# Exponentials over three PSUM banks, and the planner's queues made anew around them, in a fused attention and spectral filter kernel

## Chip, cores and metric

The kernel runs on one core of a Trainium2 chip. The metric is the time of one execution on the device in microseconds (us). TensorE is called PE below, ScalarE ACT, VectorE DVE, GpSimd POOL and SyncE, which issues most DMAs, SP.

## What is computed

Two independent halves, written side by side into one output of 2048 x 1280:

```python
# A: filter in the frequency domain, x is (1, 2048, 640)
X = rfft2(x.astype(float32))
y = irfft2(X * (w_r + 1j * w_i), s=(S, D)).astype(bfloat16)

# B: attention, 32 heads of 20, sequence 2048
qkv = (x @ wqkv).reshape(B, S, 3, H, Dh).transpose(2, 0, 3, 1, 4)
scores = einsum("bhqd,bhkd->bhqk", q, k) * Dh ** -0.5
o = einsum("bhqk,bhkd->bhqd", softmax(scores), v)
out_b = o.transpose(0, 2, 1, 3).reshape(B, S, D) @ wo
```

## The kernel before

**Tiles.** Attention goes in 32 units: 4 blocks of 512 queries times 8 groups of 4 heads. A unit has 64 tiles of scores, 16 blocks of 128 keys times 4 heads, 2048 in all. A tile is one matmul of 128 keys by 512 queries over 20 (padded to 32) rows, `score_mm` (L880), and fills one of the eight PSUM banks. The four heads of a group lie in four row groups of the PE array, so that tiles of different heads can be computed side by side, in one wave. The exponential of a tile is taken by one of two engines:

- ACT takes it exactly, two tiles in two neighbouring banks in one instruction of 128 x 1024 (L1615), into a ring of 22 slots in SBUF.
- DVE takes it by a bit trick: an eviction of 128 x 512 (or of a pair, 128 x 1024) into int16 (L1052), then for a batch of four tiles two passes over 128 x 2048 (L1110, L1113) and a scaling of V for that batch (L1102 on POOL, L1104 on DVE).

The products with V (L1198, "PV") come in waves of four matmuls, one per head, and a batch of DVE needs three waves where four tiles of ACT need one. Fills and all other products use different tile shapes of the PE array (32 rows by 128 columns against 128 rows by 32 columns).

**Around it** run the projections (L654 and, through the helper `cmm`, L283), the filter's matrix products in four stages (S1 to S4, L283), the normalisation, the output projection, their evictions on DVE, and POOL's additions. At the end an accuracy flag is read; a branch behind it holds a fallback that isn't executed here. It is the same in both kernels.

**Order.** Nothing is scheduled at run time. The class `KB` plans the program while it is built: `run` steps a clock of estimates, and whenever an engine is free by that clock it gives it the next piece. `step_pe1` tries, in this order, a fill for ACT (`try_act_fill`), background products (`bg_continue`, `bg_resume`, `try_bg`), PV waves (`try_pv`) and a fill for DVE alone (`try_dve_fill`). Where none fits, `keep_warm` may add a matmul with the identity that serves nothing else. `Prog` then works out the semaphores, and each engine executes its queue in order.

**Banks.** `SETS` gives ACT two pairs of banks, filled and emptied by turns; `POOLB` lists the other four, shared by DVE's tiles, by PV sums and by all background products (`bank_owner`). `try_act_fill` takes two tiles, and, where DVE has little to do, puts one or two tiles for DVE into the same wave, into shared banks. The exponential is issued in `try_exp`:

```python
SETS = ((0, 1), (2, 3))
POOLB = (4, 5, 6, 7)
...
in_ = self.ps[:, banks[0]:banks[0] + n, :].rearrange("p b n -> p (b n)")
self.put("act", lambda e: e.activation(o, in_, AF.Exp, bias=ACT_BIAS, scale=ACT_SCALE), ...
```

**Thresholds.** `POLICY` is a list of rows, each with a planner time in ns from which its values hold: how much work DVE may have waiting when it gets another tile (`DVE_BACK`, `DVE_BACK2`, and `DVE_LOW` for a fill of its own), how many PV matmuls make a group (`VMIN`), and the like (`NAMES`).

Of the kernel before, what the change touches and what calls it, by code (L numbers as in the profile page):

```python
# [260 lines left out]
NU = 32  # L261
# [45 lines left out]
class KB:  # L307
# [10 lines left out]
    SETS = ((0, 1), (2, 3))  # L318
    POOLB = (4, 5, 6, 7)
# [598 lines left out]
    DMIN = 14  # L918
# [15 lines left out]
    def try_act_fill(self):  # L934
        if self.ua >= NU:
            return False
        banks = self.SETS[self.grp]
# [4 lines left out]
        if self.P.peek("pe", w=[("ps", b) for b in banks]) > self.now:  # L942
            return False
        tiles = self.pick_set(len(banks))
# [4 lines left out]
        if self.dq and self.dve_wants(0):  # L949
            for k in (2, 1):  # L950
                alt = self.pick_set(len(banks), [t[2] for t in self.dq[:k]])
                if len(alt) == len(banks) and len({t[:2] for t in self.aq + alt}) <= 2:
                    tiles = alt
                    break
        left = sum(4 * len(q) for q in self.qs[self.ua:self.ua + 2]) + len(self.aq)
# [4 lines left out]
        bl = banks[:len(tiles)]  # L960
        rk = set()
# [35 lines left out]
        return True  # L997

# [8 lines left out]
    SOON = 1400.0  # L1007
    GGAP = 6000.0
    gat_next = 0.0
    RSV = 1200.0  # L1010
# [473 lines left out]
    def try_bg(self, room, urgent=False):  # L1484
        if not urgent and any(J.nxt < len(J.pe) for J in self.flight):
            return False
        banks = self.POOLB if self.act_started and self.ua < NU else (4, 5, 6, 7, 0, 1, 2, 3)
# [34 lines left out]
    def emit_chunk(self, J):  # L1522
# [11 lines left out]
        if J.nxt == len(J.pe):  # L1534
# [12 lines left out]
            self.dve_push(ops, done, any_=any_)  # L1547
# [52 lines left out]
    def try_exp(self):  # L1600
# [25 lines left out]
    NAMES = ('DVE_BACK', 'DVE_BACK2', 'VMIN', 'DVE_LOW', 'BMIN', 'PRP', 'DMIN', 'VGAP', 'RSH', 'SOON', 'RSV')  # L1626
    POLICY = [
# [876 lines left out]
```

## Time and profile before

| | |
|---|---|
| median of 3 runs | 713.07 us (713.04 to 713.34) |
| the profiled execution | 713.46 us |
| its span in the trace | 711.6 us |
| busy share: PE, DVE, ACT, POOL | 98%, 95%, 97%, 44% |
| exponentials on ACT | 748 of two tiles: 1496 tiles |
| tiles on DVE | 552, in 138 batches |

The profile comes from one execution, and its span is shorter than the time of that execution by what lies around the program. A busy time counts an engine as busy from an instruction's start to its end, and successive instructions overlap in it. So a stretch that is all busy can still hold losses: there the distance from one start to the next says more.

### The profile page before, as it was taken

What the parts mean: (1) busy time and instruction counts of PE and PEld (TensorE: products, weight loads), DVE (VectorE), ACT (ScalarE), POOL (GpSimd) and SP (SyncE); (2) the same over time, 40 slices, a digit from 0 to 9 for tenths busy, and PEclk for the clock granted to TensorE, in tenths of its full rate; (3) what the DMA queues carried; (4) which work ended last, traced back from release to release, by engine and by line L of the source; (5) the groups of instructions that cost most, each with busy time, mean ns of one, the idle gap of its engine ahead of it and who ended that gap; (6) DMA issues with size and microseconds to landing.
All of it is one profiled execution on the core that took longest, in us unless ns stands there. A gap on an engine that the chain in (4) does not pass through costs nothing.

```text
span 711.6 us, 24028 instructions
## 1 busy us (share of the span) xinstructions
PE 697.5 (98%) x10275; PEld 224.9 (32%) x10275; DVE 674.2 (95%) x1227; ACT 690.8 (97%) x754; POOL 313.3 (44%) x322
## 2 busy tenths in 40 slices
PE   8999999999999999999999999999999999999997
PEld 3422342433422222223233333333222322233333
DVE  2799999999999999999999999999999999999996
ACT  4999999999999999999999999999999999999994
POOL 6364432122343313135126177676555325658660
PEclk9999999999999999999999999999999999999999
DMA  9522222212213427133211111110300120022211
GB/s 168 183 67 73 70 68 63 62 30 60 58 31 94 137 81 266 28 111 92 58 44 32 60 32 40 37 46 19 112 21 25 38 69 19 11 72 58 75 43 50
DMA packets 54292, 48.07 MB, mean 68 GB/s; under 512 B 27884, under 2 KB 45678, under 8 KB 53926
## 3 DMA queue, kind: packets, MB, share of 16 engines
q1 hardware_dynamic: 51526, 44.36, 22.2%
q8 instruction: 82, 1.34, 0.8%
q0 software_dynamic: 768, 1.32, 0.8%
q10 hardware_dynamic: 1888, 0.81, 0.5%
q14 instruction: 28, 0.23, 0.1%
HBM read 26.67 MB, written 11.76 MB: 54 GB/s over the span
## 4 chain that ended last, share of the span: by engine, by line
ACT 63%; PE 33%; DMA 1%; DVE 1%; SPq 0%; issue 0%
ACT arena L1615 63%; PE ps L880 12%; PE ps L283 11%; PE ps L1198 9%; PE ps L654 1%; DMA arena<-in_B_x_dram 1%; DMA arena<-in_B_wqkv_dram 1%; DVE arena L1052 0%; SPq L591 0%; PE ps L1310 0%; DVE arena L1434 0%; DVE arena L1380 0%; DVE arena L2260 0%; PE ps L1293 0%; DVE arena L1110 0%
## 5 line engine op out<-in xcount | busy, mean ns | idle before, releaser
L1615 ACT ACTIVATE arena<-ps 128x1024 f16<-128x1024 f32 x748 | 687.5, 1097 | 8.4 <-PE ps L880 8.2
L1052 DVE TENSOR_SCALAR arena<-ps 128x512 int16<-128x512 f32 (+1 forms) x546 | 363.1, 688 | 11.4 <-PE ps L880 9.5
L880 PE MATMUL ps<-arena 32*128 32x512 bf16 x2048 | 293.2, 384 | 5.9 <-ACT arena L1615 3.7
L1198 PE MATMUL ps<-arena 128*32 128x512 f16 x3152 | 262.2, 384 | 1.0 <-DVE arena L2128 0.5
L283 PE MATMUL ps<-arena 128*32 128x512 bf16 (+7 forms) x4758 | 253.2, 307 | 0.4 <-DMA arena<-in_B_wqkv_dram 0.2
L880 PEld LDWEIGHTS ps<-arena 32*128 32x128 bf16 x2048 | 72.5, 91 | 275.7 <-ACT arena L1615 259.9
L1102 POOL TENSOR_SCALAR arena<-arena 128x96 bf16<-128x96 bf16 x95 | 59.9, 631 | 145.9 <-DVE arena L1052 104.0
L283 PEld LDWEIGHTS ps<-arena 128*32 128x32 bf16 (+2 forms) x4758 | 89.2, 95 | 98.8 <-issue 68.7
L1113 DVE TENSOR_SCALAR arena<-arena 128x2048 int16<-128x2048 int16 x138 | 94.3, 686 | 1.1 <-PE ps L1198 0.9
L1110 DVE TENSOR_SCALAR arena<-arena 128x2048 int16<-128x2048 int16 x138 | 94.4, 684 | 0.2
L1198 PEld LDWEIGHTS ps<-arena 128*32 128x32 bf16 x3152 | 62.6, 95 | 93.1 <-issue 60.3
L1249 POOL TENSOR_TENSOR arena<-arena 128x512 bf16<-128x512 f32 x30 | 44.6, 1487 | 61.9 <-DVE arena L1052 41.1
L2144 POOL TENSOR_TENSOR arena<-arena 128x644 bf16<-128x644 bf16 x32 | 47.2, 1477 | 15.9 <-DVE arena L1052 9.1
L1903 POOL TENSOR_TENSOR arena<-arena 128x319 bf16<-128x319 f32 x16 | 16.4, 1026 | 27.4 <-DVE arena L1110 11.8
L2128 DVE TENSOR_TENSOR arena<-ps,arena 128x644 bf16<-128x644 f32 (+1 forms) x34 | 27.9, 820 | 0.4 <-PE ps L283 0.3
L2223 POOL TENSOR_TENSOR arena<-arena 128x512 bf16<-128x512 f32 (+1 forms) x12 | 17.5, 1456 | 20.3 <-DVE arena L2215 19.6
L1897 POOL TENSOR_TENSOR arena<-arena 128x640 f32<-128x640 bf16 x8 | 12.3, 1541 | 31.3 <-DVE arena L744 14.6
L664 DVE TENSOR_SCALAR arena<-ps,arena 128x512 bf16<-128x512 f32 (+1 forms) x14 | 10.2, 731 | 13.9 <-PE ps L654 13.9
L1904 POOL TENSOR_TENSOR arena<-arena 128x319 bf16<-128x319 f32 x16 | 15.3, 956 | 17.9 <-DVE arena L1052 5.2
L701 DVE TENSOR_SCALAR arena<-ps 128x512 bf16<-128x512 f32 x34 | 23.1, 680 | 0.0
L1229 DVE COPY arena<-ps 128x512 f32<-128x512 f32 (+1 forms) x33 | 21.9, 667 | 0.7 <-PE ps L1198 0.6
L2280 POOL TENSOR_TENSOR arena<-arena 128x321 bf16<-128x321 f32 x16 | 16.2, 1013 | 10.6 <-DVE arena L2260 8.3
(62 smaller groups left out, 244.7 us busy)
## 6 DMA issues: line engine op xcount, KB each, us to landing
arena<-rd SPq DMA_DIRECT2D x120, 64.0 KB
out_dram<-arena SPq DMA_DIRECT2D x30, 160.0 KB
arena<-in_A_x_dram SPq DMA_DIRECT2D x16, 160.0 KB
xs<-arena SPq DMA_DIRECT2D x16, 160.0 KB
arena<-xs SPq DMA_DIRECT2D x4, 640.0 KB
arena<-arena SPq DMA_DIRECT2D x105, 20.0 KB
qsv<-arena SPq DMA_DIRECT2D x8, 256.0 KB
arena<-ct SPq DMA_DIRECT2D x2, 1024.0 KB
```

The lines of the kernel that those rows point to most:

```text
L283: inst = e.matmul(out[c:c + n], lhsT[:, c:c + n], rhs, start=start, stop=stop, tile_position=(0, c), skip_group_check=True)
L701: return lambda e, en: e.tensor_scalar(o, in_, sc, None, ALU.mult)
L880: return e.matmul(self.ps[:, bank, :], self.KT[32 * j:32 * j + 32, g, kt * 128:(kt + 1) * 128], self.QT[32 * j:32 * j + 32, g, qc % 2 * 51 ...
L1052: return e.tensor_scalar(o, in_, 0.0, 31744.0, ALU.max, ALU.min)
L1102: self.pool_op(lambda e: e.tensor_scalar(vs, vi, W1, None, ALU.mult), 430.0, r=vr, w=vk, name="vs")
L1110: return lambda e, en=None: e.tensor_scalar(Gi[:, lo:hi], Ii[:, lo:hi], SH1, 0.0, ALU.subtract, ALU.max)
L1113: return e.tensor_scalar(Ii, Ii, SH2, 0.0, ALU.subtract, ALU.max)
L1198: inst = e.matmul(self.ps[32 * j:32 * j + 32, bank, :], v_, p_, start=s_, stop=False, tile_position=(0, 32 * j), skip_group_check=True)
L1249: self.pool_op(lambda e: e.tensor_tensor(on, of, bc, ALU.mult), 1250.0, r=pk + [("bcu", u, j) for j in range(4)] + [("bc", j) for j in ran ...
L1615: self.put("act", lambda e: e.activation(o, in_, AF.Exp, bias=ACT_BIAS, scale=ACT_SCALE), 0.8333 * 512 * n + self.EXPO, r=[("ps", b) for b ...
L2128: return lambda e, en: e.tensor_tensor(o, in_, w_, ALU.mult)
L2144: self.pool_op((lambda o, x, y, op: lambda e: e.tensor_tensor(o, x, y, op))(o, x, y, op), 1400.0, r=r, w=w, name="comb")
```

## The change

The two pairs for ACT move to the banks 1, 2 and 5, 6, and the shared banks are 0, 3, 4 and 7. Each pair now has a shared neighbour on either side. `third`, called in `try_act_fill`, may add one of the neighbours in `NEXT` (bank 3 or 0 for the first pair, 4 or 7 for the second) to a pair, if DVE has at least `TRI` ns of work waiting and at least `TRB` shared banks are free at that moment: then three tiles go to ACT in one fill and one exponential of 128 x 1536. `TRP` forbids it while a PV sum waits for a bank.

Besides that, a fill waits if the next set would be needed only later than `FILL + SW + JIT` ns from then; evictions of background products get a priority `EVP` of 0 or 1 on DVE (1 before); `DVE_LOW` is 2000 by default rather than 1000; and the list `POLICY` is a new one, with five more columns.

```diff
-    SETS = ((0, 1), (2, 3))
-    POOLB = (4, 5, 6, 7)
+    SETS = ((1, 2), (5, 6))
+    POOLB = (0, 3, 4, 7)
+    NEXT = ((3, 0), (4, 7))
+    TRI = 1e9
+    TRB = 1
+    TRP = 0
...
         if self.P.peek("pe", w=[("ps", b) for b in banks]) > self.now:
             return False
+        late = max(self.free["act"], self.now) + sum(self.exp_occ(len(t[0])) for t in self.sets) - self.FILL - self.SW - self.JIT
+        if self.sets and late > self.now:
+            self.at(late)
+            return False
         tiles = self.pick_set(len(banks))
...
+        banks, tiles = self.third(banks, tiles)
...
         bl = banks[:len(tiles)]
+        for b in bl:
+            self.bank_owner[b] = "act"
...
+    ntri = 0
+    JIT = 300.0
+    EVP = 0
+
+    def third(self, banks, tiles):
+        if len(tiles) < 2 or not self.act_started or self.dve_backlog() < self.TRI or (self.TRP and self.want_pv()):
+            return banks, tiles
+        ok = [b for b in self.POOLB if self.bank_owner[b] is None and self.P.peek("pe", w=[("ps", b)]) <= self.now]
+        if len(ok) < self.TRB:
+            return banks, tiles
+        more = self.pick_set(3)
+        if len(more) < 3:
+            return banks, tiles
+        for b in self.NEXT[self.grp]:
+            if b in ok:
+                self.ntri += 1
+                return tuple(sorted(banks + (b,))), more
+        return banks, tiles
...
-        banks = self.POOLB if self.act_started and self.ua < NU else (4, 5, 6, 7, 0, 1, 2, 3)
+        banks = self.POOLB if self.act_started and self.ua < NU else self.POOLB + self.SETS[0] + self.SETS[1]
...
-            self.dve_push(ops, done, any_=any_)
+            self.dve_push(ops, done, prio=self.EVP, any_=any_)
...
-    NAMES = ('DVE_BACK', 'DVE_BACK2', 'VMIN', 'DVE_LOW', 'BMIN', 'PRP', 'DMIN', 'VGAP', 'RSH', 'SOON', 'RSV')
+    NAMES = ('EVP', 'JIT', 'TRI', 'TRB', 'TRP', 'DVE_BACK', 'DVE_BACK2', 'VMIN', 'DVE_LOW', 'BMIN', 'PRP', 'DMIN', 'VGAP', 'RSH', 'SOON', 'RSV')
...
-        (319927.85114074143, (2800.0, 1600.0, 8, 1000.0, 300.0, 2, 14, 0.0, 0.0, 1400.0, 1200.0)),
+        (340628.6383407404, (0, 300.0, 900.0, 2, 0, 2800.0, 1600.0, 8, 1600.0, 300.0, 1, 14, 0.0, 0.0, 700.0, 1200.0)),
...
-    DVE_LOW = 1000.0
+    DVE_LOW = 2000.0
```

What stands in the queues is shown at three places. On ACT, the exponentials before (L1615) from the first to the last, with what stands around them:

```order
L599 ACTIVATE arena<-arena 128x8
L1615 ACTIVATE arena<-ps 128x1024 x748
L1299 COPY arena<-ps 80x256 x2
L1380 CAST arena<-ps 128x512 x2
```

and after (L1645), the first of them:

```order
L603 ACTIVATE arena<-arena 128x8
L1645 ACTIVATE arena<-ps 128x1024 x35
L1645 ACTIVATE arena<-ps 128x1536
L1645 ACTIVATE arena<-ps 128x1024 x119
L1645 ACTIVATE arena<-ps 128x1536
L1645 ACTIVATE arena<-ps 128x1024 x48
L1645 ACTIVATE arena<-ps 128x1536
```

An exponential of 1536 columns stands alone among tens of the old size; over the whole queue there are 27 of them, 709 of 1024 columns, and a last one of 512.

On PE, in the filter's first stage, fills (L880 before) and products (L1198 PV, L283 filter and projections) before:

```order
L880 MATMUL ps<-arena 128x512 x2
L283 MATMUL ps<-arena 32x512 x4
L1198 MATMUL ps<-arena 32x512 x8
L880 MATMUL ps<-arena 128x512 x3
L1198 MATMUL ps<-arena 32x512 x8
L880 MATMUL ps<-arena 128x512 x3
L283 MATMUL ps<-arena 32x320 x8
```

and after, where the same lines are L884, L1228 and L283:

```order
L884 MATMUL ps<-arena 128x512 x3
L1228 MATMUL ps<-arena 32x512 x16
L884 MATMUL ps<-arena 128x512 x3
L1228 MATMUL ps<-arena 32x512 x4
L283 MATMUL ps<-arena 32x512 x4
L884 MATMUL ps<-arena 128x512 x3
L283 MATMUL ps<-arena 32x512 x12
```

Before, three fill matmuls are two tiles for ACT and one for DVE. After, the first three here are a triple for ACT; four waves of PV follow it instead of two or three.

At the end of the attention on PE, before, from the last fill on (the copy of the sums on DVE and the normalisation L1310 follow the last L1198):

```order
L880 MATMUL ps<-arena 128x512 x2
L1198 MATMUL ps<-arena 32x512 x20
L283 MATMUL ps<-arena 32x512 x8
L1198 MATMUL ps<-arena 32x512 x8
L283 MATMUL ps<-arena 32x512 x16
L1310 MATMUL ps<-arena 128x85 x4
```

and after, where the normalisation is L1340:

```order
L884 MATMUL ps<-arena 128x512
L1228 MATMUL ps<-arena 32x512 x8
L283 MATMUL ps<-arena 32x512 x12
L1228 MATMUL ps<-arena 32x512 x4
L283 MATMUL ps<-arena 32x512 x16
L1340 MATMUL ps<-arena 128x85 x4
```

The last fill has one tile, and the waves between it and the last PV are fewer, three of PV in all instead of seven.

## Rows read from the trace of the kernel before

**Rows 1.** The page: span, busy times, slices of the span in tenths.
```profile
span 711.6 us, 24028 instructions
PE 697.5 (98%) x10275; PEld 224.9 (32%) x10275; DVE 674.2 (95%) x1227; ACT 690.8 (97%) x754; POOL 313.3 (44%) x322
ACT  4999999999999999999999999999999999999994
PEclk9999999999999999999999999999999999999999
```

**Rows 2.** The page: the chain that ended last, by engine.
```profile
ACT 63%; PE 33%; DMA 1%; DVE 1%; SPq 0%; issue 0%
```

**Rows 3.** ACT's instructions: timeline (start, length, count), and durations by line (min/median/max).
```profile
10.42 7.64 ACT L1615 ACTIVATE arena<-ps 128x1024 f16<-128x1024 f32 x8 [6.03 <-PE ps L880]
383.64 1.02 ACT L1615 ACTIVATE arena<-ps 128x1024 f16<-128x1024 f32 x1
396.29 2.12 ACT L1615 ACTIVATE arena<-ps 128x1024 f16<-128x1024 f32 x2
699.28 1.02 ACT L1615 ACTIVATE arena<-ps 128x1024 f16<-128x1024 f32 x1
L1615 ACT ACTIVATE arena<-ps x14: 1019/1105/1192, 383.6 to 395.4; 128x1024 f16<-128x1024 f32 x14
L1615 ACT ACTIVATE arena<-ps x748: 1018/1086/1297, 10.4 to 699.3; 128x1024 f16<-128x1024 f32 x187
L1380 ACT CAST arena<-ps x2: 585/586/586, 705.3 to 705.8; 128x512 bf16<-128x512 f32 x2
L599 ACT ACTIVATE arena<-arena 128x8 bf16<-128x8 bf16 x1 | 0.2, 209 | 0.0
```

**Rows 4.** Waits: who waited for whom; total us, times, longest.
```profile
PEld ps L880 <- ACT arena L1615: 259.9, 669, 0.8
ACT arena L1615 <- PE ps L880: 8.2, 5, 6.0
PE ps L880 <- DVE arena L1052: 0.4, 1, 0.4
```

**Rows 5.** PE's timeline from 302 us: start, length, line, count.
```profile
302.02 0.39 PE L880 MATMUL ps<-arena 32*128 32x512 bf16 x2
302.34 0.62 PE L1198 MATMUL ps<-arena 128*32 128x512 f16 x8
302.89 0.39 PE L880 MATMUL ps<-arena 32*128 32x512 bf16 x3
303.21 0.83 PE L283 MATMUL ps<-arena 128*32 128x512 bf16 x12
303.98 0.39 PE L880 MATMUL ps<-arena 32*128 32x512 bf16 x3
```

**Rows 6.** Groups by line and form: count, busy us, mean ns, idle before.
```profile
L1052 DVE TENSOR_SCALAR arena<-ps 128x512 int16<-128x512 f32 x540 | 356.1, 682 | 10.9 <-PE ps L880 9.0
L1052 DVE TENSOR_SCALAR arena<-ps 128x1024 int16<-128x1024 f32 x6 | 7.3, 1216 | 0.5 <-PE ps L880 0.5
L1110 DVE TENSOR_SCALAR arena<-arena 128x2048 int16<-128x2048 int16 x138 | 94.4, 684 | 0.2
L1104 DVE TENSOR_SCALAR arena<-arena 128x96 bf16<-128x96 bf16 x43 | 8.0, 185 | 0.0
```

**Rows 7.** ACT's timeline: its longest wait after the first exponential.
```profile
19.33 1.02 ACT L1615 ACTIVATE arena<-ps 128x1024 f16<-128x1024 f32 x1 [1.26 <-PE ps L880]
```

**Rows 8.** Timeline of the tail: PE's last fill, DVE's copy of sums and last cast.
```profile
698.80 0.39 PE L880 MATMUL ps<-arena 32*128 32x512 bf16 x2
701.30 0.76 DVE L1229 COPY arena<-ps 128x256 f32<-128x256 f32 x2 [0.60 <-PE ps L1198]
707.12 0.69 DVE L1380 CAST arena<-ps 128x512 bf16<-128x512 f32 x1 [0.61 <-PE ps L283]
```

**Rows 9.** Busy time of each engine in one stretch of 20 us.
```profile
480.00:500.00 20.00, 18.88 (x265) 5.93 (x261) 19.89 (x32) 20.00 (x23) 12.72 (x11) 1.00 0.12 24
```

86 rows, old and new, of the table POLICY are left out of this document.

## The prediction

> **What bounds the kernel now.** I began with the page's busy line and slices [rows 1]: PE, ScalarE (ACT) and VectorE (DVE) all stand at 95% or more, and ACT's tenths read 9 from the second slice to the last but one. So the share of busy time names no bound, and the question is which engine sets the step. The chain of waits [rows 2] gives ACT 63% and PE 33%, and it runs through DVE for 1%.
>
> So next I read ACT's steps. The first exponential starts at 10.42, the last at 699.28 and ends at 700.30; the span ends at 711.6, a tail of 11.3 us [rows 1, 3]. That a row is busy is not enough here: one exponential shows 1018 ns at least and 1297 at most, but the next begins before it ends. In a quiet stretch 14 exponentials start from 383.64 on and the next one at 396.29: (396.29 - 383.64)/14 = 0.904 us a step [rows 3]. That is the engine's own pace. All 748 at that pace would take 747 x 0.904 = 675 us from the first start to the last; they took 688.9. **ACT loses 13.9 us**, of which only 2.2 us appear as idle (8.2 less the 6.0 before the first one, [rows 4]); the rest hides inside the overlapping records.
>
> PE explains the losses. The trace of PE at 302 us [rows 5] shows its cycle: a fill (L880), then products, then a fill. Two waves of four matmuls (x8) make a cycle of 302.89 - 302.02 = 0.87 us, three (x12) one of 303.98 - 302.89 = 1.09. A wave is thus 0.22, and a fill with the two changes of tile shape around it 0.87 - 0.44 = 0.43: 0.22 for the wave and 0.21 for the changes. ACT's step of 0.904 lies between the two cycles, so PE is on time with two waves and late with three. PE's fill in turn waits for ACT's bank: 669 times by the weight loads' row [rows 4]. Both engines run one loop with next to no slack.
>
> **What the change removes, adds and moves.** ScalarE: 709 exponentials of 1024 columns, 27 of 1536 and one of 512 stand in place of 748. That is 737 instructions instead of 748 and 2 x 709 + 3 x 27 + 1 = 1500 tiles instead of 1496: the triple exists in 27 places only, and ACT also takes one DVE batch of four tiles more. A tile more in the same instruction isn't in the trace. Bounds: the 512-column cast against the shortest exponential, (1018 - 586) = 432 ns for 512 columns, leaves a fixed part of 904 - 864 = 40 ns a step; the 8-column activation against it, (1018 - 209) x 512/1016 = 408 ns, leaves 88 [rows 3]. Then 4 x 432 - 11 x 40 = +1.3 us, or 4 x 408 - 11 x 88 = +0.7. I take **+1.3**, since the cast reads PSUM in whole banks as the exponential does. So the larger instruction in itself gains almost nothing: half of 40 ns, 27 times, is half a microsecond. (The Trainium skill, "ScalarE: Activation LUTs", under "What ACT_TABLE_LOAD costs", prices an activation with immediate scale and bias at 186 ns and 0.833 ns a column, with 93 ns of overlap back to back. That would make a step 946 ns, where the row shows 904; its fixed 93 would turn the sum into 4 x 427 - 11 x 93 = +0.7.)
>
> VectorE: by the order's counts two more single evictions, three pairs less, two passes over 2048 columns less, two small scalings of V more: 2 x 0.68 - 3 x 1.22 - 2 x 0.69 + 2 x 0.19 = -3.3 us [rows 6], and three such scalings less on POOL. DVE waits and is waited for a little everywhere, but it makes 1% of the chain [rows 2], so I cost this at **0**; the cover is PE and ACT, which end later. If that cover were gone it would be a gain of at most 3.3.
>
> PE, at the prices of [rows 5]: runs of fills fall from 740 to 716, 24 x 0.21 = -5.0. ACT's fill waves, 748 to 737: -2.4. VectorE's tiles mostly ride in ACT's fill on another row group at no wave of their own; by the planner's tally 3 tiles had a fill of their own and now 45 have (the threshold DVE_LOW goes from 1000 to 2000): +42 x 0.22 = +9.2. PV matmuls fall by 8, two waves: -0.4. Of the planner's keep-warm waves (L283, 32x512) 24 of four matmuls go: -5.3. Sum **-3.9 us**, but the keep-warm waves stood only where the planner saw a hole; without them PE has +1.4 us more to do. The clock shows no fall with 41 of them in the program [rows 1]; with 17 left I cost that at 0.
>
> What decides is how PE's work falls between ACT's fills. At these prices I counted in both orders the stretches between two ACT fills with more than 1.0 us of PE work: 179 before, 186 after. 28 of the 186 stand next to a triple, whose step of about 0.904 + 0.43 = 1.33 covers them. That leaves 158 uncovered ones: 13.9 x 158/179 = 12.3, a loss smaller by 1.6. Against that, a long stretch right behind a long one has nothing to recover with: there are 10 such pairs after, 5 before, and each costs the whole excess, 1.09 - 0.90 = 0.19, so +1.0. The planner's worst single place stays: a long run of products ahead of the fill for the exponential at 19.33 costs 1.26 us of ACT idle [rows 7], and a stretch of that size, now with VectorE fills in it, stands some exponentials later. Loss together: **-0.6**. Bounds: -3.9, if every microsecond that leaves PE is one that ACT waited for, and +4.6, the slow rival below.
>
> The late gate (JIT) orders no fill earlier than 0.85 us ahead of need by the planner's account. With one set of 0.904 in flight a bank comes free later than that anyway; it acts only beside a triple. 0, with both ends inside the loss term. The shared bank: a triple's fill has to wait until VectorE has read its third bank, 0.68 [rows 6], and behind that fill everything on PE waits, ACT first. The planner asks for a bank that is already free, so 0; its price if that fails is the slow rival.
>
> The tail. Before, after the last fill at 698.80, nine waves (x20, x8, x8) run until the last PV, and VectorE copies the sums at 701.30, 1.0 us after the last exponential's end [rows 8]. After, six waves stand there, and the last exponential has a single tile. I take -0.5 (bounds 0 and 3 x 0.22 = -0.7). At the end, two output waves that stood behind the last ScalarE copies stand ahead of them; the last cast waits 0.61 for PE at 707.12 [rows 8]. -0.4 (0 to -0.6). Together **-0.9**.
>
> Sum: 1.3 + 0 - 0.6 - 0.9 = -0.2 us on a span of 711.6. The profiled execution took 713.46, the median of the runs is 713.07; the change is put on the median: 712.9, say 713.0.
>
> **Rivals.** *No change that can be measured* (the forecast): the triple occurs 27 times in 737, and what it saves ACT spends on four more tiles. For it: the terms above, none over 1.5 us, of both signs. Against it: nearly every instruction on every engine moves, and a loop without slack answers to small things. 713.0.
>
> *Faster.* PE is what ACT waits for throughout, and the 3.9 us that PE has less to do come off the loss; the keep-warm waves that go weren't in holes of the real run. For it: 24 fewer pairs of tile changes, a third of the chain on PE [rows 2]. Against it: in 480 to 500 us PE is busy only 18.88 of 20, and ACT has no idle there at all [rows 9]: freed PE time isn't at once ACT time. 713.0 - 3.9 = 709.1.
>
> *Slower.* The shared bank. A triple's fill waits for VectorE's read of a bank that was never ACT's before, and PE carries out its queue in order: products, VectorE's fills and ACT's next pair stand behind it. It decides from the point where VectorE runs later than the planner thinks by more than the triple's lead. For it: VectorE is busy 19.9 us of 20 in such stretches [rows 9] and can't catch up. Against it: the planner uses banks of this pool for VectorE's own tiles in the same way, and PE was idle at such a fill once, for 0.4 us [rows 4]. Half of the triples late by half an eviction: 13.5 x 0.34 = 4.6, so 717.6. VectorE's own 45 fills are no such case: 37 of them stand in stretches that make less than 0.90 us of PE work with them, 6 under 0.98, two over 1.0, and these are in the count above.
>
> **How the numbers follow.** A difference under 0.2% (1.4 us) is about what a measurement of this kernel can't tell from no change. The forecast gets 0.48, the faster case 0.30, the slower one 0.22. The range goes from 710.2 to 716.2: the middle case whole, the larger part of the faster case down to 2.8 us, and of the slower one up to 3.2; a fifth is left out. Faster by over 0.2%: 0.30; within: 0.48; slower: 0.22.
>
> **What would show it.** ACT's 1536-column step at 1.33 to 1.34 in a quiet stretch, and pairs still at 0.904, would confirm the ACT term; a pair's step that changes would show that the placing of banks matters, for which I have no term. The losses: span of the starts less the instructions at their pace, 13.3 if I am right, 10 in the faster case, 17 to 18 in the slower, with the long steps at the triples. First start at 10.4; from the last exponential's end to the span's end 10.4 rather than 11.3. PE's granted clock below 1.00 in the middle would make all of it wrong, and so would ACT idle ahead of a triple, ended by PE L884 behind a VectorE read.

## The result, and the trace after

The changed kernel takes **717.25 us** (median of 4 runs, 716.76 to 717.27) where the kernel before takes 713.20 beside it: a ratio of 1.0053, 95% interval 1.0042 to 1.0065. It is slower by half a per cent. The forecast was 713.0, and the time lies 1.05 us beyond the upper end of the range.

The profiled execution after took 716.76 us. Its page answers to [rows 1]; then ACT's timeline, its groups by form, and its waits (line, waited for, total us, times, longest), which answer to [rows 3, 4]:

```profile
span 714.9 us, 23814 instructions
PE 694.4 (97%) x10171; PEld 224.9 (31%) x10171; DVE 672.3 (94%) x1226; ACT 692.1 (97%) x743; POOL 311.4 (44%) x319
ACT  4999999999999999999999999999999999999994
PEclk9999999999999999999999999999999999999999
...
10.54 2.86 ACT L1645 ACTIVATE arena<-ps 128x1024 f16<-128x1024 f32 x3 [6.14 <-PE ps L884]
...
L1645 ACT ACTIVATE arena<-ps 128x1024 f16<-128x1024 f32 x709 | 656.6, 1102 | 9.3 <-PE ps L884 8.8
L1645 ACT ACTIVATE arena<-ps 128x1536 f16<-128x1536 f32 x27 | 41.2, 1526 | 0.9 <-PE ps L884 0.9
...
ACT arena L1645 <- PE ps L884: 9.7, 6, 6.1
```

PE, DVE and ACT all have nearly the same busy time as before, and the slices look the same. The page can't show where 3.3 us went. Taking ACT's steps from start to start does. A pair's step is 0.903 us in the undisturbed places and a triple's 1.330; what the first-to-last stretch holds beyond that is loss:

| us | before | after |
|---|---|---|
| first exponential starts | 10.42 | 10.54 |
| steps at their own pace | 674.5 | 676.1 |
| loss | 14.3 | 15.9 |
| of it, 600 to 620 us | 0.26 | 2.48 |
| last exponential | 1.02 | 0.65 |
| its end to the span's end | 11.34 | 11.66 |
| span | 711.6 | 714.9 |

Outside one stretch of 20 us the loss fell by 0.6, the size predicted, but the kernel before varies by more than that from profile to profile (below). In that stretch ACT lost 2.2 us more. Its engines there, before, after, and after in a shorter piece (us, busy PE, PEld, DVE, ACT, POOL, granted clock, DMA share, GB/s):

```profile
600.00:620.00 20.00, 20.00 (x250) 5.30 (x245) 18.38 (x35) 20.00 (x23) 13.71 (x12) 1.00 0.08 20
```
```profile
600.00:620.00 20.00, 18.22 (x202) 4.86 (x199) 17.52 (x30) 18.37 (x18) 10.69 (x11) 0.91 0.08 20
609.00:612.35 3.35, 3.35 (x30) 0.64 (x22) 2.12 (x5) 2.44 (x3) 1.52 (x2) 0.50 0.00 0
```

DVE, POOL, PE and ACT of the changed kernel in that place, each in order of time:

```profile
604.10 0.68 DVE L2257 COPY arena<-ps 128x512 f32<-128x512 f32 x1
604.92 1.77 DVE L1143 TENSOR_SCALAR arena<-arena 128x2048 int16<-128x2048 int16 x1
606.62 2.47 DVE L1082 TENSOR_SCALAR arena<-ps 128x512 int16<-128x512 f32 x4
...
604.87 1.28 POOL L2265 TENSOR_TENSOR arena<-arena 128x512 bf16<-128x512 f32 x1 [2.44 <-DVE arena L2257]
...
604.03 0.83 PE L1228 MATMUL ps<-arena 128*32 128x512 f16 x12
...
606.75 0.40 PE L1228 MATMUL ps<-arena 128*32 128x512 f16 x4 [0.69 <-DVE arena L1143]
...
608.81 0.97 PE L283 MATMUL ps<-arena 128*32 128x512 bf16 x8
...
607.51 1.02 ACT L1645 ACTIVATE arena<-ps 128x1024 f16<-128x1024 f32 x1 [0.27 <-PE ps L884]
608.92 1.02 ACT L1645 ACTIVATE arena<-ps 128x1024 f16<-128x1024 f32 x1 [0.39 <-PE ps L884]
610.80 2.54 ACT L1645 ACTIVATE arena<-ps 128x1536 f16<-128x1536 f32 x2 [0.85 <-PE ps L884]
```

The pass at 604.92 is DVE's third pass over a batch of 128 x 2048 (L1143). It takes 1.77 us, where the group has 0.68 [rows 6]. POOL's product L2265 began 0.05 us ahead of it and ended at 606.15; the pass ends 0.54 later. Two things met. POOL is released by the eviction L2257, in the queue just ahead of the pass, and the pass itself began late: the next DVE instruction normally starts 0.60 behind such an eviction, and this one started 0.82 behind it, when PE's run of three waves (604.03 to 604.86) was through. That a wave of this run was what it waited for is read from the times and from the code (the third pass overwrites what a PV wave reads). Then the PV wave at 606.75 stands 0.69 us for the pass, PE's queue stands behind it, ACT is idle for 0.27, 0.39 and 0.85 us, and PE's granted clock is 0.50 (the lower of its levels) from 608.94 to 612.35, so that eight matmuls take 0.97 us in place of 0.62.

In the kernel before, the longest of the 276 passes takes 0.88 us. At 76 places a pass starts 0.15 to 0.17 us ahead of a POOL product, and there POOL's product is the one that grows, by some 0.38 us: 1.65 in place of 1.27 for those over 512 columns. Here is one (DVE, then POOL):

```profile
605.42 0.68 DVE L2215 COPY arena<-ps 65x512 f32<-65x512 f32 x1
606.02 0.68 DVE L1110 TENSOR_SCALAR arena<-arena 128x2048 int16<-128x2048 int16 x1
...
606.18 1.65 POOL L2223 TENSOR_TENSOR arena<-arena 65x512 bf16<-65x512 f32 x1 [1.63 <-DVE arena L2215]
607.80 1.27 POOL L2224 TENSOR_TENSOR arena<-arena 65x511 bf16<-65x511 f32 x1
```

**Theory 1:** which of the two starts first decides which one stalls; a lead of 0.16 us is all that protects a pass, and in the changed kernel one pass lost it, at a place where PE and then ACT wait for it. **Rivals:** the loss comes from the triples, four of which stand at the end of that stretch (the first at 610.80); or from the fall of the clock behind PE's hole; or the long pass has another cause, such as VectorE merely being late; and the rest of the 4 us is ACT's four extra tiles.

### The profile page after: what moved, and what is told of

It reads as the page before. It is cut to its first block, busy times and chain, and to the rows that moved or that the text cites. A ratio compares the mean times of both kernels' runs of the same rounds, so it can differ in the third digit from the quotient of the medians.

```text
span 714.9 us, 23814 instructions
## 1 busy us (share of the span) xinstructions
PE 694.4 (97%) x10171; PEld 224.9 (31%) x10171; DVE 672.3 (94%) x1226; ACT 692.1 (97%) x743; POOL 311.4 (44%) x319
## 3 DMA queue, kind: packets, MB, share of 16 engines
q8 instruction: 82, 1.34, 0.8%
## 5 line engine op out<-in xcount | busy, mean ns | idle before, releaser
L1645 ACT ACTIVATE arena<-ps 128x1024 f16<-128x1024 f32 (+1 forms) x737 | 688.7, 1117 | 10.1 <-PE ps L884 9.7
L1082 DVE TENSOR_SCALAR arena<-ps 128x512 int16<-128x512 f32 x545 | 359.9, 683 | 11.8 <-PE ps L884 9.7
L884 PE MATMUL ps<-arena 32*128 32x512 bf16 x2048 | 297.0, 385 | 8.0 <-ACT arena L1645 4.9
L1228 PE MATMUL ps<-arena 128*32 128x512 f16 x3144 | 258.6, 385 | 1.8 <-DVE arena L1143 0.7
L283 PE MATMUL ps<-arena 128*32 128x512 bf16 (+6 forms) x4662 | 244.8, 306 | 0.8 <-DVE arena L1082 0.4
L884 PEld LDWEIGHTS ps<-arena 32*128 32x128 bf16 x2048 | 73.9, 91 | 276.5 <-ACT arena L1645 244.1
L1132 POOL TENSOR_SCALAR arena<-arena 128x96 bf16<-128x96 bf16 x92 | 62.1, 675 | 147.8 <-DVE arena L1082 97.6
L283 PEld LDWEIGHTS ps<-arena 128*32 128x32 bf16 (+1 forms) x4662 | 88.4, 95 | 97.0 <-issue 65.1
L1143 DVE TENSOR_SCALAR arena<-arena 128x2048 int16<-128x2048 int16 x137 | 94.4, 690 | 2.4 <-PE ps L1228 2.1
L1228 PEld LDWEIGHTS ps<-arena 128*32 128x32 bf16 x3144 | 62.6, 95 | 95.2 <-issue 64.6
L2186 POOL TENSOR_TENSOR arena<-arena 128x644 bf16<-128x644 bf16 x32 | 45.0, 1408 | 18.1 <-DVE arena L2170 11.4
L1940 POOL TENSOR_TENSOR arena<-arena 128x640 f32<-128x640 bf16 x8 | 12.3, 1541 | 35.0 <-DVE arena L1134 23.7
L1946 POOL TENSOR_TENSOR arena<-arena 128x319 bf16<-128x319 f32 x16 | 17.6, 1099 | 21.2 <-DVE arena L1082 13.3
L1939 POOL TENSOR_TENSOR arena<-arena 128x640 f32<-128x640 bf16 x8 | 12.3, 1540 | 29.6 <-DVE arena L1140 15.1
L1945 POOL TENSOR_TENSOR arena<-arena 128x319 bf16<-128x319 f32 x16 | 16.4, 1027 | 17.3 <-DVE arena L1143 6.5
L2265 POOL TENSOR_TENSOR arena<-arena 128x512 bf16<-128x512 f32 (+1 forms) x12 | 16.7, 1394 | 15.6 <-DVE arena L2257 13.5
```

What stands on the lines that cost most here:

```text
L283: inst = e.matmul(out[c:c + n], lhsT[:, c:c + n], rhs, start=start, stop=stop, tile_position=(0, c), skip_group_check=True)
L884: return e.matmul(self.ps[:, bank, :], self.KT[32 * j:32 * j + 32, g, kt * 128:(kt + 1) * 128], self.QT[32 * j:32 * j + 32, g, qc % 2 * 51 ...
L1082: return e.tensor_scalar(o, in_, 0.0, 31744.0, ALU.max, ALU.min)
L1132: self.pool_op(lambda e: e.tensor_scalar(vs, vi, W1, None, ALU.mult), 430.0, r=vr, w=vk, name="vs")
L1143: return e.tensor_scalar(Ii, Ii, SH2, 0.0, ALU.subtract, ALU.max)
L1228: inst = e.matmul(self.ps[32 * j:32 * j + 32, bank, :], v_, p_, start=s_, stop=False, tile_position=(0, 32 * j), skip_group_check=True)
```

## Experiments

The runs below come from three chips, and each ran beside the kernel before. The product held back, the hole filled, the triples cut in two and the kernel without triples ran beside 712.71 us. The two tries with memsets, the kernel before again and the shortened exponentials ran beside 712.70. The two with the longer delay, and the changed kernel with the second run of the held-back product, ran beside 713.43.

### The one product held back

```diff
         self.run()
+        self.P.order["pool"][256].deps.append(self.P.order["dve"][1032])
```

> The changed kernel with one wait more and nothing else: the POOL addition that started at 604.87 us, 50 ns ahead of a DVE pass over 2048 columns, now waits for the end of that pass. Theory 1 (the pass of 1774 ns, where its kind takes 690, held back PE's next products, ACT lost 1.0 us and then, under PE's clock at 0.50 from 608.9 to 612.4, another 1.3): the pass takes 0.69, no stretch of low clock before the end, ACT's loss in 600 to 620 us falls from 2.5 to about 0.3, and the median from 717.25 to 715.0. Theory 2 (the low clock has nothing to do with the pass, but with 24 keep-warm waves less): the clock still falls near 609 us, median 716.2 or more. Theory 3 (the triples and their shared banks cost the time, and the pass is hidden): 717 as it is.

Measured: 714.07 us, ratio 1.0017 (1.0007 to 1.0027), profiled span 711.7. DVE's pass and the stretch:

```profile
604.49 0.70 DVE L1143 TENSOR_SCALAR arena<-arena 128x2048 int16<-128x2048 int16 x1
...
607.50 1.25 DVE L1140 TENSOR_SCALAR arena<-arena 128x2048 int16<-128x2048 int16 x1
...
600.00:620.00 20.00, 18.80 (x232) 5.64 (x232) 18.95 (x34) 20.00 (x21) 10.72 (x10) 1.00 0.07 21
```

ACT has no idle in the stretch, its loss there is 0.43 us in place of 2.48, the clock stays at 1.00, and the triples are still there. Two thirds of the slowdown went with one wait between two engines. A collision is left: the pass at 607.50 takes 1.25 us, since POOL's next product (606.92) leads it by 0.57. PE shows no wait behind this one, and ACT doesn't idle. So a long pass by itself is not the price; the price is paid where PE and ACT wait for it.

### The hole filled, the collision left

Three waves that add zero stand ahead of the PV wave that waits for the late pass, so that PE isn't idle there.

```diff
+        if len(self.P.order["pe"]) == self.HOLE:
+            self.fill_hole(bank)
```

> The changed kernel with the late pass left as it is, and three waves of matmuls that add zeros to the PV sums put ahead of the products that wait for it, so that PE works in that hole (with one small memset on DVE at the start). If the hole in PE's work is what lowers the clock: the clock stays at 1.00, ACT still loses about 1.0 us ahead of 609 us but not the 1.3 behind it, median about 716.0. If the clock falls for another reason: it is 0.50 for 3.4 us again, and the median is 717.3. If the hole is not hidden by the waves and they only push everything back, 717.5 and more.

Measured: 716.35 us, 1.0054 (1.0037 to 1.0070). The granted clock of the stretch is 1.00, and ACT still loses 2.1 us there, since three more waves don't make the pass shorter and a second pass now collides (DVE, then POOL):

```profile
609.78 1.79 DVE L1145 TENSOR_SCALAR arena<-arena 128x2048 int16<-128x2048 int16 x1
...
609.75 1.27 POOL L1298 TENSOR_TENSOR arena<-arena 128x512 bf16<-128x512 f32 x1 [1.29 <-DVE arena L2271]
```

In the changed kernel the low clock had moved this second pass to 611.78, when POOL's product (610.66 to 611.93) was nearly through, and it took 0.70. So the clock is not what the time hangs on: without its fall the same stretch costs nearly as much in another way. Over all four profiles with the first collision, ACT loses 2.5 us there with the fall and 1.9 to 2.1 without it, then with a second collision.

### The triples cut in two

The same order, each triple issued as an exponential of 1024 and one of 512 columns.

```diff
+        if n == 3:
+            o3, i3 = o[:, 1024:1536], in_[:, 1024:1536]
+            t3 = self.P.add("act", lambda e: e.activation(o3, i3, AF.Exp, ...), ...)
```

> The changed kernel in the same order on every engine, with each of the 27 exponentials of 1536 columns issued as one of 1024 and one of 512: what the larger instruction saves by itself. By the steps in the trace (903 ns for two banks, 1330 for three) the fixed part is 903 - 2 x 427 = 49 ns, so 27 x 0.05 = 1.3 us if ACT sets the end at each of them: 718.5. If triples stand where ACT waits anyway, under 0.3: 717.3. If splitting frees the first two banks sooner and that helps PE, a gain: 716.5.

Measured: 717.78 us, 1.0068 (1.0051 to 1.0084); the interval overlaps that of the changed kernel. ACT's steps say it more sharply: the single behind a pair starts at 384.82, the next exponential at 385.30.

```profile
384.82 0.76 ACT L1651 ACTIVATE arena<-ps 128x512 f16<-128x512 f32 x1
385.30 35.12 ACT L1647 ACTIVATE arena<-ps 128x1024 f16<-128x1024 f32 x38
```

A triple cut in two costs 0.903 + 0.48 = 1.38 us against 1.330: the triple itself saves 0.05 us, 27 times, 1.35 us (the steps at their pace sum to 677.5 here, 676.1 with triples). The loss in the stretch is still 1.85 us, with the hole of 0.69 us in PE, a second late pass (1.79 us at 611.70) and no fall of the clock. So the long exponentials don't cause it. The fills into three banks are still there in this run, but they were there with the product held back as well, and the loss wasn't. Such a hole isn't always followed by the low clock.

### No triples, planned anew

```diff
     def third(self, banks, tiles):
+        return banks, tiles
```

> The changed kernel with the triple switched off in the planner, which then makes all queues anew with the new banks and the new list of thresholds. The list was made for an order with triples, so it fits worse whatever the triple is worth. Theory 1 says nothing on the size; the losses must show in ACT's steps at places that the rows name, and if a POOL addition and a pass start together there, in a pass of over 1 us. If the triples themselves cost the 4 us, this is faster than 717.25. I expect slower, 718 to 724.

Measured: 718.64 us, 1.0081 (1.0064 to 1.0098), ACT's work 676.3. The profile is of the slowest of its four runs, 721.76 us. ACT's loss is 20.9 us there. The granted clock is 0.50 from 14.77 to 21.60, and ACT loses 3.9 in the first 20 us, about 1 in other profiles. The largest single hole:

```profile
307.07 1.94 ACT L1646 ACTIVATE arena<-ps 128x1024 f16<-128x1024 f32 x2 [4.21 <-PE ps L1229]
```

The thresholds in `POLICY` were made for an order with triples; with the triples gone the planner builds another order, with a stall of 4.2 us of its own, while PE has a run of 84 products (L283, 302.53 to 306.45) ahead of the PV wave that ACT waits for. This run says how far one order differs from the next, and nothing on the triple.

### The collision put into the kernel before: a try that missed

Four memsets of one column directly ahead of four passes (600.2, 606.0, 611.5, 617.6 us), or, as a control, one instruction earlier, ahead of the eviction that releases POOL.

```diff
+        for k, i in enumerate((1024, 1034, 1043, 1053)):
+            late(k, order[i])          # control: order[i - 1]
...
+                    e.memset(scr[:, i:i + 1], 0.0)
```

> The kernel before, with four tiny memsets (one column each, about 0.06 us apiece, some 0.25 us together) put on VectorE directly ahead of four passes at 600.2, 606.0, 611.5 and 617.6 us. In the kernel before each of these passes starts 0.16 us ahead of a GpSimd product that the eviction ahead of the pass releases; with the memsets GpSimd should start about 0.1 us ahead of the pass. Theory (who starts first decides): the passes take about 1.75 us in place of 0.68, the GpSimd product 1.27 in place of 1.64, and the time is 0.7 to 4 us longer, by how many of the four reach ScalarE. Rival (a pass of 1.77 us has another cause, such as the late matmul wave ahead of it): passes stay at 0.68 us and the time grows by 0 to 0.3 us.

> The kernel before, with the same four memsets at the same four places, but one instruction earlier on VectorE, ahead of the eviction that releases GpSimd: eviction, GpSimd product and pass are all about 0.25 us later, and the pass still starts 0.16 us ahead of GpSimd. Theory: passes 0.68 us, products 1.64 us as before, time within 0.5 us of the kernel before. Rival (lateness of VectorE by itself is what costs): the same loss as with the memsets behind the eviction.

Measured: 712.88 us, 1.0004 (0.9994 to 1.0013), and 712.64, 1.0000 (0.9990 to 1.0009). All passes stay at 0.68. The row of the memsets shows why:

```profile
605.47 0.06 DVE L2464 MEMSET scr<- 128x1 f32 x1
605.47 0.68 DVE L1110 TENSOR_SCALAR arena<-arena 128x2048 int16<-128x2048 int16 x1
605.48 0.07 DVE L2464 MEMSET scr<- 128x1 f32 x3
...
605.60 1.69 POOL L2223 TENSOR_TENSOR arena<-arena 65x512 bf16<-65x512 f32 x1 [1.63 <-DVE arena L2215]
```

A row reads 0.06 us, but back to back the four delay the pass by some 0.03 us together. I had added up lengths of records where the step from start to start counts. The lead was kept, so this tells nothing of theory 1.

### The kernel before, again

> The kernel before, unchanged, as a yardstick on this chip: ratio 1.000 within 0.002 and a profiled span of 711.3 to 711.9 us, if the chips differ little; the spans of the other runs of this chip are read against it.

Measured: 712.74 us, ratio 1.0000 (0.9990 to 1.0009), span 710.4. The kernel before varies by itself: over its five profiles (its own, this one, the two tries above and the control below, which leave ACT's order as it is) ACT's loss is 13.4 to 14.3 us.

### The collision put into the kernel before: with a longer delay

The same places, one reduction over 256 columns in place of the memsets.

```diff
+                e.tensor_reduce(scr[:, k:k + 1], one.to_broadcast([128, 256]), AX.X, ALU.add)
```

> The kernel before, with one small reduction (256 columns, about 0.3 us) on VectorE directly ahead of the same four passes at 600.2, 606.0, 611.5 and 617.6 us; the four memsets of the earlier try delayed the passes by only some 0.02 us, so that they still started first. The delay is now longer than the 0.16 us of lead. Theory (who starts first decides): GpSimd starts 0.1 to 0.2 us ahead, the four passes take about 1.6 to 1.75 us in place of 0.68 and the products 1.27 in place of 1.64; time 0.7 to 4 us longer. Rival (a long pass has another cause): passes stay at 0.68 us and the time grows by 0 to 0.5 us.

> The kernel before, with the same four reductions one instruction earlier, ahead of the eviction that releases GpSimd: the same work and the same lateness on VectorE, but the pass keeps its 0.16 us of lead. Theory: passes 0.68 us, products 1.64 us, time within 0.6 us of the kernel before. Rival (lateness of VectorE by itself is what costs): the same loss as with the reductions behind the eviction.

Measured: **715.86 us, 1.0032** (1.0022 to 1.0042) with POOL first, **713.62, 0.9999** (0.9990 to 1.0009) for the control, which has the same work and the same lateness. POOL first, the site at 600 us (DVE, then POOL):

```profile
599.86 0.69 DVE L2215 COPY arena<-ps 128x512 f32<-128x512 f32 x1
600.47 0.41 DVE L2464 TENSOR_REDUCE scr<-arena 128x1 f32<-128x256 f32 x1
600.80 1.66 DVE L1110 TENSOR_SCALAR arena<-arena 128x2048 int16<-128x2048 int16 x1
...
600.64 1.27 POOL L2223 TENSOR_TENSOR arena<-arena 128x512 bf16<-128x512 f32 x1 [1.69 <-DVE arena L2215]
```

The control, the site at 606 us (DVE, then POOL):

```profile
605.36 0.68 DVE L2215 COPY arena<-ps 65x512 f32<-65x512 f32 x1
605.95 0.68 DVE L1110 TENSOR_SCALAR arena<-arena 128x2048 int16<-128x2048 int16 x1
...
606.12 1.65 POOL L2223 TENSOR_TENSOR arena<-arena 65x512 bf16<-65x512 f32 x1 [1.96 <-DVE arena L2215]
```

Between 600 and 640 us ACT loses 3.1 us in the first and 0.9 in the control, a difference of 2.2; the medians differ by 715.86 - 713.62 = 2.24. So lateness alone costs little (0.9 us lost against 0.6 in the kernel before, and nothing in the medians), and the order of the two starts costs 2.2 us. Three of the four sites collided, and a further pass, at 609.70, met POOL's next product and took 1.06 us. Theory 1 holds in a kernel that has neither triples nor new banks. The fourth site went the other way (DVE, then POOL):

```profile
607.16 0.68 DVE L1110 TENSOR_SCALAR arena<-arena 128x2048 int16<-128x2048 int16 x1
...
607.00 1.98 POOL L2223 TENSOR_TENSOR arena<-arena 65x512 bf16<-65x512 f32 x1 [1.64 <-DVE arena L2215]
```

There POOL also began 0.16 us earlier by its record, and yet the pass ran through and POOL stalled. This product covers 65 partitions, the three others 128. That alone is not the reason: in the kernel without triples a product over 65 partitions that led by 0.50 us did hold a pass up (1.31 us at 540.62). POOL's product ends 1.14 us behind the pass here, as it does where the pass leads (1.13 at 606 us in the kernel before), so it behaved as the second to start, whatever its record says. Why stays open.

### ScalarE's work made shorter

```diff
+        m = 512 * n - (16 if self.nexp > 12 and n == 2 else 0)
+        o2, i2 = o[:, 0:m], in_[:, 0:m]
```

> The kernel before, with every two-bank exponential after the twelfth over 1008 columns in place of 1024 (the last 16 queries of the second tile are left out and keep old values), all else as it is. About 735 steps are shorter by 16 columns; one bank of 512 columns costs 427 ns (1330 less 903), so 13.3 ns each and 9.8 us in all. Theory (ScalarE's work reaches the end one to one, so the 1.6 us that the changed kernel adds to it are paid in full): 702.5 to 705 us where the kernel before has 713. Rival (TensorE or VectorE are as close behind as ScalarE is): only 0 to 5 us come off, and ScalarE's idle time grows by the rest; then the added 1.6 us were only partly paid.

Measured: 709.45 us, 0.9957 (0.9940 to 0.9974): 3.25 us less, where ACT's steps are shorter by 9.5 (0.890 in place of 0.903). ACT's first-to-last stretch went from 688.1 us (the kernel before, again) to 684.6, and its loss from 13.5 to 19.6. The rival expectation holds: two thirds of what ACT gains is waited away, which fits PE's cycle: 0.87 us with two waves [rows 5], only 0.02 below the new step. ACT's group of shortened exponentials:

```profile
L1618 ACT ACTIVATE arena<-ps 128x1008 f16<-128x1008 f32 x736 | 672.2, 1032 | 1.2 <-PE ps L880 0.9
```

### The changed kernel, and the held-back product, on one chip

> The changed kernel with the one GpSimd product at 604.9 us held back until the pass beside it is done, a second time, now beside the changed kernel itself on one chip. Theory (the one late pass costs 2 to 2.5 us, ScalarE's added 1.6 us of work the rest): 713.8 to 714.8 where the kernel before has 712.7, and 2 to 3 us under the changed kernel. Rival (the difference of the first comparison came from the chip): within 1 us of the changed kernel.

> The changed kernel, unchanged, on this chip. Theory: ratio 1.004 to 1.0065 to the kernel before; a pass of over 1.7 us at 604.9 us in the profile again, since the order of the instructions leaves only some 0.05 us between the two starts. Open: whether TensorE's granted clock falls at 609 us again; where it does not, the theory still has ScalarE lose about 2 us between 600 and 620 us.

Measured: 714.43 us, 1.0019 (1.0009 to 1.0029), and 717.20, 1.0048 (1.0030 to 1.0066): by the medians one wait is worth 2.8 us. The changed kernel's second profile (DVE, then POOL, then the stretch in which the clock had fallen, and one at the start):

```profile
605.35 1.76 DVE L1143 TENSOR_SCALAR arena<-arena 128x2048 int16<-128x2048 int16 x1
...
610.99 1.79 DVE L1143 TENSOR_SCALAR arena<-arena 128x2048 int16<-128x2048 int16 x1
...
605.29 1.27 POOL L2265 TENSOR_TENSOR arena<-arena 128x512 bf16<-128x512 f32 x1 [2.43 <-DVE arena L2257]
...
610.96 1.27 POOL L1279 TENSOR_TENSOR arena<-arena 128x512 bf16<-128x512 f32 x1 [1.29 <-DVE arena L2252]
...
609.00:612.35 3.35, 3.30 (x36) 0.84 (x36) 3.24 (x5) 2.94 (x3) 1.94 (x2) 1.00 0.00 0
7.80:11.10 3.30, 3.25 (x64) 2.19 (x60) 1.20 (x3) 0.00 (x0) 1.20 (x2) 0.50 0.76 155
```

The collision is there again, 0.06 us apart. The clock stays up at this place, and the second pass collides in its place; ACT loses 1.9 us in the stretch. With the first product held back, the span is 712.1 and ACT's loss 13.6.

The spans of these two profiles differ by 3.0 us, and not all of that is the collision. In the changed kernel's profile the granted clock was 0.50 from 7.72 to 11.13, ahead of the first exponential, which starts at 12.01 instead of 10.59; ACT loses 0.9 less behind it, so 0.5 remains. Between 600 and 640 us ACT loses 2.25 against 0.61: 1.6 us for the collisions. The last 0.8 lies behind the last instruction that computes, where SP waits for the last transfers to land. SP's waits of the first changed profile, then of the first with the product held back (total us, times, longest):

```profile
SPq L217 <- DMA out_dram<-arena: 1.7, 3, 1.2
```
```profile
SPq L217 <- DMA out_dram<-arena: 1.1, 3, 0.5
```

In the first pair of profiles (spans 714.9 and 711.7, a difference of 3.2) the shares are 2.2 us between 600 and 640, 0.5 in the landing, and 0.4 between 300 and 400 us. So what is shown of the collision is 1.6 to 2.2 us of ACT's time. Whether the late landing, 1.2 to 1.5 us at the longest in all four profiles with the first collision and 0.5 in both without, has to do with it stays open.

## Why the prediction was wrong, step by step

**The step that failed: VectorE at nothing.** I costed DVE at 0 on the ground that "the cover is PE and ACT, which end later", and read its waits as 1% of the chain [rows 2]. The price of a pass was taken as fixed at 0.69 us. It isn't: it depends on whether POOL's product or the pass begins first, and the change lays both anew. I counted the stretches of PE between ACT's fills and never the order of DVE's passes against POOL's products. The trace of before shows the other half of the fact, POOL products of 1.65 us beside others of 1.27 on the same form, and I had no row of POOL at all. The term put at 0 is 2.8 us by the medians where the two kernels ran beside each other (717.20 - 714.43); in the profiles 1.6 to 2.2 of it are ACT's loss at that place, and the rest has no shown tie to it.

Of the signs that the prediction named against itself, two came in part. The granted clock fell in the middle, once, at 608.94, after the holes in PE and not before them. And ACT was idle ahead of a triple, 0.85 us at 610.80, ended by PE L884; but PE was late there from the PV wave that waited for a pass, and not from VectorE's read of a third bank.

**The slow rival** had the right idea in its condition, "VectorE runs later than the planner thinks", and 717.6 is close to the time, but its place was wrong. PE's wait for DVE's read at a fill was 0.4 us before [rows 4] and 1.2 after:

```profile
PE ps L884 <- DVE arena L1082: 1.2, 3, 0.8
```

The triple's step stays at 1.330 us. Of the 2.48 us lost in the stretch some 2.1 are lost at pairs ahead of its first triple, behind the PV wave that waits for a pass and in the low clock after it. That the number fits is luck.

**ScalarE's work** was right: triple 1.330 (predicted 1.33 to 1.34), pair 0.903, so the banks' placing doesn't change it. Steps +1.6, last exponential -0.37: +1.2 against +1.3.

**The loss** came out at 13.4 and 13.6 with the product held back, against 13.3 predicted. I give this little weight. The kernel before scatters from 13.4 to 14.3, which is more than the 0.6 that I forecast, and the two figures don't rest on one pace: at the 0.903 us a step used here the loss before is 14.3 and not the prediction's 13.9, so that 0.6 less would be 13.7.

**The tail** was forecast too good, by about 0.7 and more. From the last exponential to the span's end the held-back kernels take 11.13 and 11.16 us, the kernel before 11.34 to 11.53: -0.2 to -0.3, where -0.9 was forecast. The changed kernel itself takes 11.66 and 11.99, which is longer than before; its engines run as in the held-back kernels, and the difference is the landing shown above. The first half came nearly as said (sums copied 0.67 us behind the last exponential instead of 1.00). The second didn't. Four waves of products (16 matmuls, 707.07 to 707.94) that stood behind the flag's product now stand ahead of it, DVE waits 1.50 us for that product instead of 0.62, and its last additions and casts stand behind it, after and before:

```profile
708.40 0.15 DVE L1481 TENSOR_REDUCE arena<-ps 1x1 f32<-1x5 f32 x1 [1.50 <-PE ps L1477]
...
709.92 0.68 DVE L1410 CAST arena<-ps 128x512 bf16<-128x512 f32 x1
```
```profile
704.91 0.15 DVE L1451 TENSOR_REDUCE arena<-ps 1x1 f32<-1x5 f32 x1 [0.62 <-PE ps L1447]
```

From the end of ACT's last copy (707.54) to the end of the last cast are 3.06 us, 2.89 before: +0.17 where I had -0.4.

**PE's 3.9 us less** gave nothing that can be told from the scatter, against the fast rival.

**What is left** without the collision is 1.0 us by medians beside the changed kernel (714.43 - 713.43) and 1.4 in the first comparison (714.07 - 712.71). In the profiles of the former (spans 712.1, and 711.5 for the control) it is: first start +0.4, steps +1.6, loss -0.8, last exponential -0.4, tail -0.2, in all +0.6. How much of the added 1.6 is paid can't be separated from the loss: the shortened exponentials show that of time taken from ACT only a third arrives. So this last 1.0 to 1.4 us is described and not explained.

The rule behind the collision is in the Trainium skill, "SBUF — State Buffer", section "Who interferes with whom": VectorE in its two-port modes and GpSimd take a shared pair of ports for a whole instruction, and whoever issues first makes the other wait; "Issue order, not op shape, decides who blocks." The runs agree at all places shown but the one at 607.16; no row names the mode of a pass.

## What to carry to other kernels

Where a planner or a hand-made order puts VectorE passes over SBUF and GpSimd products side by side, look for the pairs whose starts lie within a few tenths of a microsecond, and ask which one must not stall: a wait on the other engine, where GpSimd has time to spare, cost nothing here and was worth 2.8 us by the medians. When a change re-plans everything, price an instruction by what runs beside it and not by the mean of its group. A late pass is not dear by itself: one of 1.25 us cost nothing where no other engine waited for it. And when three engines are at 95%, an engine with 1% of the chain can still set the time, at a single place.

## What the hardware showed that was not expected

- A pass that finds POOL's product running ends 0.54 to 0.56 us after the product does, wherever in it the pass began: 1.77 us when POOL led by 0.05, 1.66 at 0.16, 1.25 at 0.57, 1.06 at 0.76, 0.79 at 1.03. Alone it takes 0.68.
- The other way round POOL's product grows by less, from 1.27 to 1.65 us.
- TensorE's granted clock fell to 0.50 for 3.4 us in the first profile of the changed kernel, after PE had stood 0.69 and 0.21 us; in the second profile, with the same first hole, it didn't. There it was 0.50 from 7.72 to 11.13 us instead, after PE had stood 2.02 us for a transfer, and the first exponential came 1.5 us later than in the first profile. What decides that stays open.
- Four one-column memsets in a row, 0.06 us each by their records, delay the next instruction by 0.03 us together.
